# One-query attention with gradients: loads and stores described in runs of 8 KB

## The chip, the cores and the metric

The kernel runs on one core of one Trainium2 chip. The metric is the device time of one execution in microseconds. Seven executions of the kernel before took 1304.75 to 1309.08 us, median 1306.13.

The core has TensorE (matrix products, called PE in the profile; its weight loads have a row of their own, PEld), VectorE (DVE), ScalarE (ACT), GpSimd (POOL) and SyncE (SP). Sixteen transfer engines move data between the chip's large memory (DRAM) and the on-chip memory SBUF, which has 128 partitions. A transfer is started by an instruction on SyncE or GpSimd and then runs by itself; a semaphore tells when all of it has landed. The transfer engines carry it out in packets, and the profile has a record of each.

## The reference

Attention of one query per head over 8192 keys, forward and backward:

```python
B, H, Sq, Sk, D = 2, 32, 1, 8192, 128      # bfloat16
scores = einsum("bhqd,bhkd->bhqk", q, k) * D ** -0.5
p      = softmax(scores)
out    = einsum("bhqk,bhkd->bhqd", p, v)
dq, dk, dv = vjp(grad_out)                  # gradients of q, k and v
```

There are 64 heads. `k`, `v`, `dk` and `dv` each hold 134 MB, so 268 MB are read and 268 MB written. Everything else is small. With `P` the probabilities and `dS` the gradient of the scores, a row of `dv` is `P` times `grad_out`, and a row of `dk` is `dS` times `q`: both are outer products of a long vector and a vector of 128.

## The kernel before

**Tiles.** Two heads that follow one another in memory form a pair; there are 32 pairs. The 16384 rows of a pair's `k` (or `v`) are laid over the 128 partitions, 128 rows to each, so partitions 0 to 63 hold the first head and 64 to 127 the second. A row has 128 elements of 2 bytes, so a partition's share is 32 KB. It is one contiguous run in DRAM and one contiguous run in the partition, and the whole tile `kvt` is 4 MB. The view of DRAM in this form is made at line 67 (`g p n d`: pair, partition, row, element).

**Buffers.** SBUF has room for six such tiles (`NTILE`), so for three pairs. `slot_of` (line 80) gives the tile of pair i the buffer that pair i-3 used. The gradient is written over the input in the same buffer: `dv` over `v` and `dk` over `k` (`outer`, line 426). A buffer's life is therefore load, compute, overwrite, store, and then the load of a tile three pairs later.

**Transfers.** `load` (line 85) starts loads on SyncE, one transfer of 4 MB for a tile. The very first tile comes in four pieces of 1, 1, 2 and 4 chunks of 16 rows a partition (0.5, 0.5, 1 and 2 MB). `outer` starts the stores on GpSimd (line 446), one transfer of 4 MB when the last of a tile's eight chunks has been overwritten. The last pair's stores are cut finer: `dv` in two of 2 MB, `dk` in pieces of 2, 1, 0.5 and 0.5 MB (`last_v` and `last_k`, lines 453 and 454). Neither engine does much else, and each works through its transfers in program order. A load waits until the store of the tile before it in its buffer has landed.

**Work on a tile.** For a chunk of 16 rows a partition, TensorE transposes 16 blocks of 128 x 128 (line 183), ScalarE copies them out (line 185), and TensorE multiplies them with the query or with `grad_out` (line 194). That gives the scores and the products with `grad_out`. VectorE and ScalarE turn them into `P` and `dS` in steps between chunks (lines 203 to 363). TensorE then accumulates the output and `dq` over the same rows (line 376), VectorE gathers the accumulators (`pick`, line 385) and writes the outer products into the tile (line 432).

**Order.** The order of the work is written by hand. The loop at line 457 runs over chunks, 16 to a pair, and starts each stage of the earlier pairs at a fixed distance behind the transposes. Every instruction is pinned to this order on its engine (`pin`). The loads of pair i+3 are issued in the loop after the last outer product of pair i (lines 469 to 472).

Of the kernel before, what the change touches and what calls it, by code (L numbers as in the profile page):

```python
# [17 lines left out]
NG = 2  # L18
GH = 2
NTILE = 6  # L20


@with_exitstack
def kernel(
# [27 lines left out]
    load_eng = nc.sync  # L52
    store_eng = nc.gpsimd
    pin = tc.keep_in_program_order
# [25 lines left out]
    def slot_of(i, w):  # L80

        n = 2 * i + w
        return n if n < NTILE else slot_of(i - NTILE // 2, 1 - w)

    def load(i, w, pieces=(NCH,)):
        h = pairs_[i]
        t = kvp.tile([P, NT, D], BF16, tag=f"kv{slot_of(i, w)}", name="kvt")
        h.tile[w] = t
        src = (v_v if w else k_v)[i]
        c = 0  # L90
        for m in pieces:
            n0, n1 = c * CH, (c + m) * CH
            pin(load_eng.dma_start(out=t[:, n0:n1, :], in_=src[:, n0:n1, :]))  # L93
            c += m

    load(0, 0, (1, 1, 2, 4))

    qd_nat = evp.tile([P, CH, P], BF16, tag="ev", name="qd_nat")
    for w, a in enumerate((q, grad_out)):
        pin(load_eng.dma_start(out=qd_nat[:BH, w, :], in_=a.rearrange("b h s d -> (b h s) d")))  # L100

    load(0, 1)
    for j in range(1, min(NTILE // 2, NP)):
        load(j, 0)
        load(j, 1)
# [17 lines left out]
    for g in groups:  # L123
# [3 lines left out]
            out=par[g : g + CW], in_=rows.rearrange("p b h -> p h b"), axis=AX.X  # L127
# [298 lines left out]
    def outer(i, w, c, ends):  # L426

        h = pairs_[i]
        n0 = c * CH
        shape = [P, CH, D // 2, 2]  # L430
        pin(
            nc.vector.tensor_tensor(  # L432
                out=h.tile[w][:, n0 : n0 + CH, :].rearrange("p n (e t) -> p n e t", t=2),
                in0=h.qb[w][:]
                .rearrange("p (e t) -> p e t", t=2)
                .unsqueeze(1)
                .to_broadcast(shape),
                in1=h.pair[w][:, n0 : n0 + CH, :].unsqueeze(2).to_broadcast(shape),
                op=ALU.mult,
            )  # L440
        )
        if c + 1 in ends:
            at = ends.index(c + 1)
            b0, b1 = (ends[at - 1] if at else 0) * CH, (c + 1) * CH
            dst = (dv_v if w else dk_v)[i]
            pin(store_eng.dma_start(out=dst[:, b0:b1, :], in_=h.tile[w][:, b0:b1, :]))  # L446

    A1 = NCH + 4
    O1 = A1 + 1
# [7 lines left out]
    for g in range(SL * NP + O0 + NCH + 4 - SL):  # L457
# [15 lines left out]
        if x := within(O1):  # L473
            outer(x[0], 1, x[1], last_v if x[0] == NP - 1 else whole)
        if x := within(O0):
            outer(x[0], 0, x[1], last_k if x[0] == NP - 1 else whole)
# [77 lines left out]
```

## Time and profile before

| | |
|---|---|
| median of seven executions | 1306.13 us |
| lowest and highest | 1304.75 and 1309.08 us |
| the profiled execution, its time | 1309.08 us |
| the profiled execution, its span | 1307.3 us |
| read from DRAM, written to DRAM | 268.47 MB, 268.47 MB |
| store of a tile, from issue to landing (median) | 39.9 us |
| load of a tile, from issue to landing (median) | 27.8 us |
| store instruction on GpSimd, line 446 (median) | 0.53 us |
| load instruction on SyncE, line 93 (median) | 0.33 us |

The span runs from the first instruction that the profiler sees to the last; the time is what the device reports for the execution. A profile page lists the busy time of each engine, then the span in 40 slices with one digit per slice for the busy share in tenths, then the transfer queues. Queue q1 carries what SyncE starts (descriptors generated in hardware) and q0 what GpSimd starts (descriptors written by software). A queue's share is the time of its packets as a part of sixteen engines' span. Packets can overlap a little on an engine, so a share over a short stretch can exceed 1.

The compute that costs most stands in these groups; columns are line, engine, operation, tiles written and read, shapes and count, then busy time in all, mean of one, and idle time of the engine just before them with what ended it:

```profile
L185 ACT COPY ev<-tp 128x2048 bf16<-128x2048 bf16 x512 | 954.5, 1866 | 289.9 <-PE tp L183 272.1
L183 PE MATMUL tp<-ident_bf,kvt 128*128 128x128 bf16 x8192 | 584.4, 228 | 124.4 <-DMA kvt<-in_k_dram 63.1
L432 DVE TENSOR_TENSOR kvt<-qb,pair 128x2048 bf16<-128x2048 bf16 x512 | 615.4, 1219 | 50.7 <-PE acc L376 47.7
```

TensorE's transposes wait 63.1 us for loads of `k` to land, and others for loads of `v`.

### The profile page before, as it was taken

The numbers are of one execution on the slowest core, as the hardware profiler recorded it, in microseconds if no ns is written. First come the engines' busy times: TensorE is split into PE (matmuls) and PEld (weight loads), VectorE is DVE, ScalarE is ACT, GpSimd is POOL, SyncE is SP. The second block draws the span as 40 slices with busy tenths as digits, with TensorE's granted clock in tenths as the row PEclk, the third lists the DMA queues.
The fourth block names the chain that finished last, engine by engine and source line by source line (L and its number), as shares of the span: only waits on it lengthen the run. The fifth ranks groups of instructions, "written<-read, shape, count | busy, mean of one in ns | idle before, by whom it ended". The sixth has DMA issues, their size and how long they took to land.

```text
span 1307.3 us, 41375 instructions
## 1 busy us (share of the span) xinstructions
PE 1144.3 (88%) x19108; PEld 847.5 (65%) x19108; DVE 850.9 (65%) x1551; ACT 984.9 (75%) x641; POOL 37.4 (3%) x76
## 2 busy tenths in 40 slices
PE   4999998888988989889898898888888989889893
PEld 4777776666766766666666666666666667667661
DVE  0688775656756667666675675656667657577566
ACT  5899987777877868777787787777777768678770
POOL 0000000000000000000000000000000000000000
PEclk9999998989989989899898998989899889899886
DMA  9999999999999999999999999999999999999968
GB/s 400 427 366 428 429 430 430 430 430 430 427 414 426 427 422 413 410 423 419 414 405 426 412 418 415 417 413 417 421 411 418 421 420 415 423 415 417 422 268 340
DMA packets 19933, 539.58 MB, mean 413 GB/s; under 512 B 2480, under 2 KB 2480, under 8 KB 2992
## 3 DMA queue, kind: packets, MB, share of 16 engines
q1 hardware_dynamic: 9968, 268.51, 49.5%
q0 software_dynamic: 9792, 268.44, 48.3%
q8 instruction: 149, 2.44, 0.7%
q14 instruction: 24, 0.20, 0.0%
HBM read 268.47 MB, written 268.47 MB: 411 GB/s over the span
## 4 chain that ended last, share of the span: by engine, by line
issue 69%; DMA 22%; PE 5%; POOL 2%; DVE 1%; SPq 0%; ACT 0%; POOLq 0%; DVEq 0%; ACTq 0%
DMA kvt<-in_v_dram 19%; DMA out_dram<-kvt 3%; PE tp L183 2%; POOL out_dram L446 2%; PE acc L376 1%; DVE kvt L432 1%; PE dpw L194 1%; PE sw L194 0%; ACT ev L185 0%; DVE sel L399 0%; POOLq L446 0%; SPq L93 0%; SPq L100 0%; PE sw L222 0%; PE sw L211 0%
## 5 line engine op out<-in xcount | busy, mean ns | idle before, releaser
L185 ACT COPY ev<-tp 128x2048 bf16<-128x2048 bf16 x512 | 954.5, 1866 | 289.9 <-PE tp L183 272.1
L183 PE MATMUL tp<-ident_bf,kvt 128*128 128x128 bf16 x8192 | 584.4, 228 | 124.4 <-DMA kvt<-in_k_dram 63.1
L432 DVE TENSOR_TENSOR kvt<-qb,pair 128x2048 bf16<-128x2048 bf16 x512 | 615.4, 1219 | 50.7 <-PE acc L376 47.7
L183 PEld LDWEIGHTS <-kvt 128*128 128x128 bf16 x8192 | 504.2, 103 | 134.5 <-DMA kvt<-in_k_dram 65.5
L194 PEld LDWEIGHTS <-ev 128*128 128x128 bf16 x8192 | 239.9, 96 | 218.6 <-issue 135.2
L376 PE MATMUL acc<-kvt,dS_pad 128*64 128x512 bf16 x1024 | 169.6, 416 | 1.6 <-DVE dS_pad L362 1.6
L376 PE MATMUL acc<-kvt,E_pad 128*64 128x512 bf16 x1024 | 170.3, 415 | 0.0
L194 PE MATMUL sw<-qdT,ev 128*128 128x2 bf16 x4096 | 142.1, 164 | 2.6 <-ACT ev L185 2.5
L194 PE MATMUL dpw<-qdT,ev 128*128 128x2 bf16 x4096 | 142.0, 164 | 1.0 <-ACT ev L185 1.0
L270 DVE CUSTOM_DVE_ANT_0 junk<-E_f,dpw 64x128 bf16<-64x128 f32 x64 | 18.3, 285 | 125.8 <-PE dpw L194 125.4
L207 DVE TENSOR_REDUCE mp<-sw 64x1 f32<-64x128 f32 x64 | 18.5, 289 | 125.0 <-PE sw L194 124.5
L446 POOL DMA_DIRECT2D out_dram<-kvt x68 | 36.3, 534 | 1258.5 <-DVE sel L393 647.7
L399 DVE SCALAR_TENSOR_TENSOR sel<-acc,diag,sel 128x128 f32<-128x128 f32 x192 | 67.3, 351 | 6.8
L376 PEld LDWEIGHTS <-dS_pad 128*64 128x64 bf16 x1024 | 37.9, 111 | 29.5 <-issue 6.4
L376 PEld LDWEIGHTS <-E_pad 128*64 128x64 bf16 x1024 | 37.2, 111 | 26.2 <-issue 5.1
L262 DVE CAST E_pad<-E_f 64x128 bf16<-64x128 f32 x64 | 15.3, 239 | 48.5 <-ACT E_f L252 48.5
L413 PE MATMUL acc<-par,sel 128*128 128x2 f32 x128 | 21.9, 241 | 10.1 <-DVE sel L399 10.1
L413 PEld LDWEIGHTS acc<-par,sel 128*128 128x128 f32 x128 | 19.7, 195 | 10.9 <-DVE sel L399 10.9
L176 DVE CAST qb<-dpw 128x128 bf16<-128x128 f32 x64 | 18.2, 284 | 13.1 <-PE dpw L167 13.1
L252 ACT ACTIVATE E_f<-sw,negm 64x128 f32<-64x128 f32 x64 | 23.2, 362 | 1.6
L352 DVE SCALAR_TENSOR_TENSOR dSu<-dpw,negdelta,E_f 64x128 f32<-64x128 f32 x64 | 22.4, 350 | 2.2
L393 DVE TENSOR_SCALAR sel<-acc,diag 128x128 f32<-128x128 f32 x64 | 22.3, 348 | 1.0
(49 smaller groups left out, 215.1 us busy)
## 6 DMA issues: line engine op xcount, KB each, us to landing
out_dram<-kvt POOLq DMA_DIRECT2D x62, 4096.0 KB, 39.9
kvt<-in_v_dram SPq DMA_DIRECT2D x32, 4096.0 KB, 27.8
kvt<-in_k_dram SPq DMA_DIRECT2D x31, 4096.0 KB, 27.9
out_dram<-kvt POOLq DMA_DIRECT2D x3, 2048.0 KB, 8.7
kvt<-in_k_dram SPq DMA_DIRECT2D x1, 2048.0 KB, 11.5
kvt<-in_k_dram SPq DMA_DIRECT2D x2, 512.0 KB, 4.4
kvt<-in_k_dram SPq DMA_DIRECT2D x1, 1024.0 KB, 6.8
out_dram<-kvt POOLq DMA_DIRECT2D x1, 1024.0 KB, 7.6
```

Of the source, the lines that this page charges most:

```text
L183: pin(nc.tensor.transpose(tp[:, t, :], src[:, c * CH + t, :], ident_bf[:]))
L185: pin(nc.scalar.copy(out=ev[:], in_=tp[:]))
L194: nc.tensor.matmul(dst[:, c * CH + t, :], lhsT=ev[:, t, :], rhs=qdT[:, w, GH * i : GH * (i + 1)], start=True, stop=True,)
L207: pin(nc.vector.reduce_max(out=h.mp[hs], in_=h.s[hs, :, g], axis=AX.X))
L252: nc.scalar.activation(out=h.E_f[hs], in_=h.s[hs, :, g], func=ACT.Exp, bias=h.negm[hs], scale=scale, accum_out=h.ld[hs, g : g + 1],)
L352: nc.vector.scalar_tensor_tensor(out=dSu[hs], in0=h.dp[hs, :, g], scalar=negdelta[hs], in1=h.E_f[hs], op0=ALU.add, op1=ALU.mult,)
L376: nc.tensor.matmul(h.acc[w][g : g + CW, :], lhsT=wts[:, n0 * GH : n0 * GH + CW], rhs=rows[:, n0 : n0 + QT, :].rearrange("p n d -> p (n d)" ...
L393: nc.vector.tensor_scalar(out=h.sel[:], in0=block, scalar1=diag[:, 0:1], scalar2=None, op0=ALU.mult)
L399: nc.vector.scalar_tensor_tensor(out=h.sel[:], in0=block, scalar=diag[:, b : b + 1], in1=h.sel[:], op0=ALU.mult, op1=ALU.add,)
L413: nc.tensor.matmul(h.acc[w][:, 0:GH], lhsT=h.sel[:], rhs=par[:], start=True, stop=True)
L432: nc.vector.tensor_tensor(out=h.tile[w][:, n0 : n0 + CH, :].rearrange("p n (e t) -> p n e t", t=2), in0=h.qb[w][:] .rearrange("p (e t) -> ...
L446: pin(store_eng.dma_start(out=dst[:, b0:b1, :], in_=h.tile[w][:, b0:b1, :]))
```

## The change

`max_dma_last_dim` caps the last dimension of a transfer's description, in bytes; a longer run is split into several of that length. The default is 64 KB, so a partition's 32 KB were one run. The change sets 8 KB for the tiles' loads and for their stores. A 4 MB transfer is then described as 128 x 4 x 4096 elements in place of 128 x 16384, with 512 runs in place of 128; a 2 MB transfer goes from 128 runs of 16 KB to 256 of 8 KB. Transfers of 1 MB and less have runs of 8 KB or 4 KB and stay as they are. The bytes, the addresses, the number of transfers, their order and their semaphores are the same, and no other instruction differs. The loads of `q` and `grad_out` and the stores of the two small outputs keep the default.

```diff
+RUN_L = 8192
+RUN_S = 8192
...
-            pin(load_eng.dma_start(out=t[:, n0:n1, :], in_=src[:, n0:n1, :]))
+            pin(
+                load_eng.dma_start(
+                    out=t[:, n0:n1, :], in_=src[:, n0:n1, :], max_dma_last_dim=RUN_L
+                )
+            )
...
-            pin(store_eng.dma_start(out=dst[:, b0:b1, :], in_=h.tile[w][:, b0:b1, :]))
+            pin(
+                store_eng.dma_start(
+                    out=dst[:, b0:b1, :], in_=h.tile[w][:, b0:b1, :], max_dma_last_dim=RUN_S
+                )
+            )
```

## The prediction

> **What bounds the kernel now.** I read the shares of the engines first, then the transfer lines of the page, then its stages, then the waits of SyncE's queue, and at last the trace's transfer records (start, duration, size and queue of every packet).
>
> ```profile
> PE 1144.3 (88%) x19108; PEld 847.5 (65%) x19108; DVE 850.9 (65%) x1551; ACT 984.9 (75%) x641; POOL 37.4 (3%) x76
> DMA  9999999999999999999999999999999999999968
> DMA packets 19933, 539.58 MB, mean 413 GB/s; under 512 B 2480, under 2 KB 2480, under 8 KB 2992
> q1 hardware_dynamic: 9968, 268.51, 49.5%
> q0 software_dynamic: 9792, 268.44, 48.3%
> ```
>
> TensorE looks busiest by its share, but the transfer engines are busy in every slice until the last two: loads (q1) take 49.5% of sixteen engines' span and stores (q0) 48.3%. By stages:
>
> ```profile
> 20.00:56.00 36.00, 33.50 (x623) 26.95 (x621) 14.29 (x30) 33.54 (x22) 0.00 (x0) 0.95 1.00 428
> ...
> 180.00:700.00 520.00, 463.57 (x7697) 342.57 (x7696) 341.05 (x620) 396.27 (x259) 13.83 (x26) 0.92 1.00 422
> 700.00:1220.00 520.00, 455.95 (x7571) 337.17 (x7567) 336.95 (x607) 389.40 (x252) 13.29 (x25) 0.92 1.00 417
> 1220.00:1260.00 40.00, 36.21 (x617) 26.72 (x614) 26.51 (x48) 31.68 (x21) 1.06 (x2) 0.93 0.92 388
> 1260.00:1271.00 11.00, 11.00 (x177) 8.30 (x174) 7.31 (x16) 8.92 (x9) 0.10 (x1) 0.88 0.21 86
> 1271.00:1307.30 36.30, 14.83 (x169) 8.35 (x168) 24.99 (x42) 5.66 (x4) 3.62 (x7) 0.71 0.84 348
> ```
>
> The last two columns are the busy share of the transfer engines and GB/s. From 180 to 1220 us that share is 1.00 while TensorE has 56 and 64 us to spare. The transfer engines stand idle in earnest in one place, between 1260 and 1271, when the last pair is computed and there is nothing to move. The queue waits close the ring:
>
> ```profile
> SPq L93 <- DMA out_dram<-kvt: 1184.7, 58, 60.0
> ...
> POOL out_dram L446 <- DVE sel L393: 647.7, 32, 24.3
> ```
>
> A load waits for the store of the tile that it overwrites (1185 us in 58 waits), so more transfer time delays every later load. The chain of waits calls 69% of the span "issue", with no cause; I trust the transfer share instead. The kernel is bound by the time its transfer packets take.
>
> **What one packet costs.** The 4 MB transfers are 128 runs of 32 KB, and the records show one packet for a run: 8064 load and 7936 store packets of 32 KB, 1000 of them per engine. Neighbours on an engine overlap by 3 to 4 ns, so I use the median step from start to start. Other sizes stand in the same trace, because the first loads and the last stores are cut smaller:
> - loads: 32 KB 1209.5 ns, 16 KB 607, 8 KB 306 (305.7 without rounding, from a duration of 309 and the overlap), 4 KB 152.
> - stores, measured where stores alone run, mostly after the last load: 32 KB 1215 ns, 16 KB 613, 8 KB 314.5 (mean 318.3), 4 KB 160.
>
> From load packets, 32 KB in four runs costs 4 x 305.7 = 1222.8 ns against 1209.5: **13.3 ns dearer**, or 4.4 ns for each added packet. In the body, store packets behave as loads do: both have a median of 1213 ns there, a step from load to store is 1210, and one from store to load 1209, so changing direction costs at most 1 ns.
>
> The Trainium skill ("DMA: Bandwidth & Descriptors", section "Why small descriptors are slow") names about 3 cycles per packet; at the 850 MHz of that page this is an estimate of 3.5 ns, 3 x 3.5 x 1000 = 10.6 us in the sum below, where the rows make it 13.3.
>
> **Which engine paces.** Between 100 and 1220 us, 445 of 7153 store packets, one in sixteen, take 1225 to 1450 ns (mean 1304). Chained by end and start they are one engine, alternating stores near 1310 and loads near 1229: (1310 + 1229)/2 - 3.5 = 1266 ns a packet. All engines together start 6335 packets of 32 KB from 700 to 1200 us, one per engine in 500,000 x 16/6335 = 1263 ns. So the slow engine sets the pace late in the body; from 140 to 290 us, with queued work still in hand, it is 1228. The others lose the difference when they run out of loads and begin the next together: 921 load packets take over 1250 ns, and all load packets together exceed 1213 by 23.9 us per engine. What stretches the slow engine follows the instructions: store packets during which fewer than 5 instructions start are longer by 29 ns on average, those with 65 or more by 140. That goes by time and not by packet, and stays.
>
> The same skill page ("Latency and other measured facts") says that engines 7 and 15 are usually slow and guesses at the descriptor rings of software transfers. The trace agrees that one engine is slow. By that guess the stretch would grow with the descriptors, and the sum would be that of the third rival; by the count of instructions it adds nothing.
>
> **The change, part by part.**
> - Loads: 63 of 4 MB go from 128 packets to 512, one of 2 MB from 128 to 256; the 512 KB and 1 MB pieces have runs of 8 KB or less already. 504 per engine x 13.3 ns = 6.7 us.
> - Stores: 62 of 4 MB and 3 of 2 MB likewise; the last three are untouched. 496 x 13.3 = 6.6 us by the load rows; by the store-only rows 496 x (1258 - 1215 = 43) = 21.3 us, and by their mean 28.8. I take the load row: those store rows come from a stretch in which all engines store at once, while in the body the 32 KB store is at the load's 1213.
> - Cover: none, up to the last load's landing near 1256 us, as the share is 1.00 through the body; after it 199 store packets of 32 KB are left (12 per engine), so the dearer row adds there at most 12 x 43 ns = 0.5 us, and the idle 1260 to 1271 us swallows part of it.
> - Issue on GpSimd: a store instruction takes 0.53 us for 128 runs, and no row shows more runs. Bounds: 0 and three times as much again, 1.6 us. It hides: a store lands 39.9 us after issue, though 8 packets alternating with loads need 16 x 1.263 = 20.2, so it waits behind another store for some 19 us. Without that cover it is 1.6 us per store, 65 times 1.6 = 104 us at the very worst. The last, small stores keep their form.
> - Issue on SyncE: 0.33 us, bound likewise 0 to 1.0 us more per load. Loads land after 27.8 us against 20.2 of work: 7.6 us of queue hide it. SyncE has nothing else behind it but the next load, which waits for a store.
> - No semaphore, buffer, order or compute instruction changes. The landing of a transfer is still the moment when its last packet is done.
>
> Sum: 6.7 + 6.6 = 13.3 us. The profiled execution took 1309.08 us around a span of 1307.3; it becomes some 1320.6 in span and 1322.4 in time. It lies 2.95 us above the median of the seven runs, 1306.13, so I forecast 1306.1 + 13.3 = **1319.4 us**, 1.0% slower.
>
> **Rivals.**
> 1. *Shorter runs remove the load stalls (faster).* When the engines start a load together, packets take up to 2.9 us; alternating with stores every 8 KB could spread them. If all of the 23.9 us went and decided the end: 1306.1 + 13.3 - 23.9 = 1295.5 us. Against: partitions and addresses keep their order, the 4 KB loads at the start have such first packets too (801, 726, 1215 ns), and while the slow engine paces, the others' stalls cost nothing. It decides once more than 13.3 us of stall is both removed and on the path.
> 2. *Stores at the dearer row.* 6.7 + 21.3 = 28.0 us, 1334 us; by the mean row 35.5 us, 1342. For it: that is how 8 KB stores were seen.
> 3. *The slow engine's stretch goes by the packet.* Its stores run 1310 - 1213 = 97 ns over; four packets would each pay that, 3 x 97 x 496 = 144 us more: 1306 + 13 + 144 = 1463 us. Against: store packets of 16 KB and 8 KB at the end have medians of 615 and 316, 4 and 7 ns over the loads' 611 and 309, though few instructions run then.
> 4. *It does nothing*: the runs adjoin in both memories, and descriptor generation could merge them, or the packets' cost could be hidden: 1306 us. Against: the changed program's transfers carry 128x4x4096 elements where they had 128x16384, and every packet size in the trace is the last dimension of its transfer.
>
> **How the numbers follow.** Forecast (1314 to 1328) 0.58; dearer stores 0.15; per-packet stretch 0.02; nothing 0.10; stalls removed 0.15. Within 0.2% (2.6 us, about what a measurement of this kernel can tell from no change) is the fourth rival: same 0.10; faster 0.15; slower 0.75. The range, 1302 to 1337, takes in the forecast, no change, half of the second rival and the nearer third of the first, and leaves out about 2 in 10. The forecast's own range is 1314 to 1328.
>
> **What would show it.** Right: about 68,000 packets, with 34,300 on q1 and 34,000 on q0; load packets of 309 ns; the share still 1.00 from 180 to 1220 us; about 418 and 413 GB/s in the two long stages; the last load landing some 13 us later and the tail after it unchanged. Store packets near 316 instead of 309 mean the second rival; loads without packets over twice the median, and a span under 1307, the first; as many packets as before, the fourth. The prediction is wrong if GpSimd's or SyncE's instructions grow by more than their queues hide, which would show as a share below 1.00 in the body.

## The result and the profile after

The changed kernel takes 1311.03 us (median of 15 runs, 1310.1 to 1312.83) against 1307.63 us for the kernel before, run beside it (median of 35, 1304.75 to 1310.5). The ratio is 1.0027, 95% interval 1.002 to 1.0034: slower, by some 3.4 us. The forecast was 1319.4 us, slower by 13.3. The side was right and the size was not. The profiled execution took 1312.37 us around a span of 1310.6 us.

The transfer lines of the page and the same six stages as before (the last columns are PE clock, busy share of the transfer engines, GB/s):

```profile
DMA packets 68445, 539.58 MB, mean 412 GB/s; under 512 B 2480, under 2 KB 2480, under 8 KB 2992
q1 hardware_dynamic: 34288, 268.51, 49.8%
q0 software_dynamic: 33984, 268.44, 48.9%
```

```profile
20.00:56.00 36.00, 33.08 (x646) 26.59 (x643) 15.18 (x32) 34.73 (x23) 0.25 (x1) 1.00 1.01 417
180.00:700.00 520.00, 460.70 (x7591) 340.56 (x7593) 335.63 (x609) 390.32 (x254) 18.61 (x25) 0.92 1.01 421
700.00:1220.00 520.00, 460.61 (x7634) 340.01 (x7632) 341.30 (x617) 393.98 (x257) 19.34 (x26) 0.92 1.01 413
1220.00:1260.00 40.00, 36.38 (x597) 26.88 (x597) 26.30 (x48) 30.41 (x20) 1.49 (x2) 0.91 1.01 417
1260.00:1271.00 11.00, 9.34 (x137) 6.76 (x138) 3.99 (x9) 6.84 (x8) 0.00 (x0) 0.84 0.61 258
1271.00:1310.60 39.60, 21.38 (x242) 12.10 (x239) 28.53 (x49) 9.36 (x6) 4.51 (x7) 0.69 0.79 324
```

The packets became what they were meant to be: 34,288 and 33,984 in place of 9968 and 9792. The loss shows where only loads run (417 GB/s against 428) and late in the body (413 against 417). From 180 to 700 us it is barely there (421 against 422). At the end the picture turns round. Between 1220 and 1271 us the transfer engines had room before (0.92 and 0.21 busy) and are busier now (1.01 and 0.61). Work that came late fell into time that had been idle.

The trace's transfer records tell how much. Tiles of 4 MB that the engines had moved, loads and stores together (a packet under way counts by the part of its time that has passed):

```
time in the span, us     before     after    behind
 600                      59.74     59.42     0.32
 900                      89.32     88.93     0.39
1140                     113.13    112.54     0.59
1230                     122.03    121.33     0.70
1260                     124.76    124.27     0.49
1270                     125.00    124.95     0.05
```

Late in the body a 4 MB tile takes 10.1 us (8 packets per engine at 1263 ns), so 0.70 tiles are 7.1 us. By 1230 us the forecast's price came to 13.0 us (122 tiles x 8 packets per engine x 13.3 ns), so little more than half of it shows. By 1270 us nearly all of the lag is caught up, because the old kernel's transfers had run dry. Of the delay 3.3 us of span is left, carried by the compute after the last load. The chain of waits names that load in both kernels (start, duration):

```profile
1223.08 33.63 DMA kvt<-in_v_dram
```

```profile
1233.71 27.90 DMA kvt<-in_v_dram
```

The first line is the kernel before, the second the changed one. The load starts 10.6 us later, but takes 5.7 us less, and lands at 1261.6 instead of 1256.7 us: 4.9 us later, where the prediction had some 13. From the end of the last load packet to the end of the span it was 52.1 us and is now 49.8; the prediction had that tail unchanged.

GpSimd's store instructions did grow. The line's view (minimum, median and maximum in ns) now reads 743 ns for 512 runs; with 128 runs it was 531. Before and after:

```profile
L446 POOL DMA_DIRECT2D out_dram<-kvt x68: 531/531/673, 56.7 to 1295.9; - x68
```

```profile
L453 POOL DMA_DIRECT2D out_dram<-kvt x68: 532/743/885, 55.7 to 1299.7; - x68
```

### The profile page after: what moved, and what is told of

It reads as the page before. It is cut to its first block, busy times and chain, and to the rows that moved or that the text cites. A ratio compares the mean times of both kernels' runs of the same rounds, so it can differ in the third digit from the quotient of the medians.

```text
span 1310.6 us, 41375 instructions
## 1 busy us (share of the span) xinstructions
PE 1151.0 (88%) x19108; PEld 851.0 (65%) x19108; DVE 850.7 (65%) x1551; ACT 984.8 (75%) x641; POOL 51.1 (4%) x76
## 3 DMA queue, kind: packets, MB, share of 16 engines
q1 hardware_dynamic: 34288, 268.51, 49.8%
q0 software_dynamic: 33984, 268.44, 48.9%
## 4 chain that ended last, share of the span: by engine, by line
issue 86%; DMA 7%; POOL 3%; DVE 1%; PE 1%; SPq 0%; POOLq 0%; ACT 0%; DVEq 0%; ACTq 0%
DMA kvt<-in_v_dram 4%; DMA out_dram<-kvt 3%; POOL out_dram L453 3%; DVE kvt L438 1%; PE tp L189 1%; PE acc L382 0%; PE dpw L200 0%; POOLq L453 0%; ACT ev L191 0%; DVE sel L405 0%; SPq L96 0%; SPq L106 0%; PE acc L419 0%; DVE dSu L358 0%; DVE sel L399 0%
## 5 line engine op out<-in xcount | busy, mean ns | idle before, releaser
L382 PE MATMUL acc<-kvt,E_pad 128*64 128x512 bf16 x1024 | 173.8, 423 | 0.0
L453 POOL DMA_DIRECT2D out_dram<-kvt x68 | 50.1, 736 | 1248.5 <-DVE kvt L438 620.7
L182 DVE CAST qb<-dpw 128x128 bf16<-128x128 f32 x64 | 18.2, 284 | 13.6 <-PE dpw L173 13.6
L346 DVE TENSOR_SCALAR negdelta<-dpw,rl 128x1 f32<-128x1 f32 x32 | 7.0, 218 | 27.2 <-PE dpw L306 27.1
## 6 DMA issues: line engine op xcount, KB each, us to landing
kvt<-in_v_dram SPq DMA_DIRECT2D x32, 4096.0 KB, 27.8
kvt<-in_k_dram SPq DMA_DIRECT2D x31, 4096.0 KB, 27.9
kvt<-in_k_dram SPq DMA_DIRECT2D x1, 2048.0 KB, 11.4
```

What stands on the lines that cost most here:

```text
L382: nc.tensor.matmul(h.acc[w][g : g + CW, :], lhsT=wts[:, n0 * GH : n0 * GH + CW], rhs=rows[:, n0 : n0 + QT, :].rearrange("p n d -> p (n d)" ...
```

## The experiments

Each run was timed against the kernel before on the same chip; ratios compare these. Between chips the kernel before itself differs, with medians from 1306.81 to 1309.88 us, so a difference of 2 or 3 us between runs on two chips is read by ratios or left undecided. Where the text says "late", it means a packet's duration over the undisturbed one of its size (159, 309, 611 and 1213 ns for 4, 8, 16 and 32 KB), from the transfer records.

**One side alone.** Two kernels set one constant of the change and leave the other at 32 KB.

```diff
-RUN_S = 8192
+RUN_S = 32768
```

> Loads in 8 KB runs, stores in 32 KB runs. Theory A (the added packets cost 4.4 ns each on the path, 13.3 us for both sides; fewer load stalls give about 6 us of it back, and idle transfer time at the end hides about 3): half of the packets, 6.7 us, is added. And the engines alternate queues packet by packet, so stores take four times the bytes of loads while both wait; the last load lands later against the stores, and the idle time at the end grows: 1310 to 1322 us. Theory B (the packets' cost lies beside slack of the engines and only the issue of stores on GpSimd, 0.53 to 0.74 us, is on the path): stores keep their form, so 1306 to 1308 us.

```diff
-RUN_L = 8192
+RUN_L = 32768
```

> Stores in 8 KB runs, loads in 32 KB runs. Theory A: 6.7 us more for the packets, but loads now take four times the bytes of stores while both wait, so the last load lands earlier and more of the stores fall into the idle time at the end (about 11 us): 1298 to 1309 us, and a larger store backlog when the last load lands than the 3.3 tiles of before. Theory B (only the issue of stores on GpSimd is on the path): the whole difference of the change, 1310 to 1312 us.

Short loads alone took 1324.36 us, ratio 1.0122 (1.0097 to 1.0147), a little above theory A's range. Short stores alone took 1308.80 us, 0.9995 (0.9982 to 1.0008), just inside theory A's. Theory B falls on both: the store instructions were 533 ns in the slow one and 743 ns in the one that costs nothing. The lists of transfers show the other half, the sharing between queues (last column: us from issue to landing). Short loads first, then short stores:

```profile
out_dram<-kvt POOLq DMA_DIRECT2D x62, 4096.0 KB, 18.0
kvt<-in_v_dram SPq DMA_DIRECT2D x32, 4096.0 KB, 46.2
```

```profile
out_dram<-kvt POOLq DMA_DIRECT2D x62, 4096.0 KB, 49.9
kvt<-in_v_dram SPq DMA_DIRECT2D x32, 4096.0 KB, 18.8
```

Before, they were 39.9 and 27.8. An engine takes a packet from each queue in turn, whatever its size, so the side with longer runs gets its bytes through first. The records show it between 150 and 300 us, wherever an engine's packets can be followed by their ends and starts: with short loads exactly one load of 8 KB stands between two stores of 32 KB (662 times of 662, where sharing by bytes would put four), and with short stores exactly one store between two loads (596 of 597). With short loads the tiles arrive late, TensorE loses 8 us between 60 and 180 us (111.99 us busy against 119.92), and the last load lands at 1266 us. The stretch from 60 to 180 us, in the kernel before and with short loads:

```profile
60.00:180.00 120.00, 119.92 (x2137) 89.57 (x2136) 94.55 (x171) 110.53 (x75) 3.72 (x7) 1.00 0.98 413
```

```profile
60.00:180.00 120.00, 111.99 (x1962) 83.75 (x1960) 85.52 (x155) 101.22 (x68) 3.19 (x6) 0.96 0.99 411
```

With short stores the last load lands at 1253 us and 4.2 tiles are left to store in place of 3.7. They use the idle time at the end (share 0.67 from 1260 to 1271 us, where it was 0.21), and that can pay for the added packets; no run separates it.

**Other lengths on both sides.**

```diff
-RUN_L = 8192
-RUN_S = 8192
+RUN_L = 4096
+RUN_S = 4096
```

> Loads and stores in 4 KB runs, seven added packets for each 32 KB in place of three. Theory A: 4.4 ns x 7000 = 31 us more work per engine, less 6 to 10 us of stalls and 3 us of cover at the end: 1323 to 1330 us. Theory B (packets hidden, issue on GpSimd on the path): the store instruction grows again by some 0.3 us, so 1312 to 1316 us.

```diff
-RUN_L = 8192
-RUN_S = 8192
+RUN_L = 16384
+RUN_S = 16384
```

> Loads and stores in 16 KB runs, one added packet for each 32 KB. Theory A: 4.4 us more work per engine; if the relief of the stalls goes with the length of the runs it may give 2 to 5 back: 1304 to 1310 us. Theory B: 1307 to 1309 us, with store instructions of 0.6 us.

4 KB: 1322.37 us, 1.0099 (1.0081 to 1.0116), 0.6 us below theory A's range and well above B's. 16 KB: 1304.89 us, 0.9966 (0.9951 to 0.998), *faster* than before and inside theory A's range alone. Run again on another occasion:

> The whole kernel with loads and stores in runs of 16 KB once more, on another chip perhaps. Theory C: below the kernel before by 2 to 6 us, a ratio of 0.995 to 0.999, as the slow engine's pace says (5.5 us). Rival: the gain seen once was the chip's or the runs' spread: a ratio of 1.000 to 1.004, as the price of the packets alone would give (5.6 us).

1304.13 us, 0.9962 (0.9946 to 0.9977): inside theory C's range, though the pace that was its reason does not hold up (below). The gain of 0.3 to 0.4% is there on both chips. The records show what shorter runs give back. Loads over 250 ns late, and what they add per engine:

```
runs              such loads    us per engine    all lateness, loads + stores, us per engine
32 KB                575            20.9              24.6 + 9.0
16 KB                505            16.7              22.1 + 6.4
16 KB, again         500            17.1              22.4 + 6.1
 8 KB                391            12.8              19.3 + 7.8
 4 KB                 32             0.8               5.2 + 16.1
 8 KB, loads only    376             9.4              19.8 + 12.8
 8 KB, stores only   355            11.3              15.8 + 15.4
```

The two runs with 16 KB agree to 0.1 us in all lateness. With one side short the sum hardly falls (33.6 to 32.6 and 31.2): the loads are less late and the stores later.

If the stalls are on the path, the transfers should lag by the added price less the lateness that went. The price here uses the undisturbed steps of these traces: 1209.4, 607.1, 305.9 and 155.3 ns for 32, 16, 8 and 4 KB, so 32 KB cost 4.7, 14.1 and 33.0 ns more in the three shorter lengths. All in us per engine, up to 1230 us of the span, against the kernel before:

```
runs      price    lateness that went    price less that    lag measured
16 KB       4.6           5.0                -0.4            -1.1 (both runs)
 8 KB      13.8           7.0                 6.8             7.1
 4 KB      32.2          13.2                19.0            15.9
```

For 16 and 8 KB the last two columns agree within a microsecond, for 4 KB within some 3.

**The price of a packet by itself.** All computation is left out; every tile is loaded and stored again.

```diff
-    load(0, 0, (1, 1, 2, 4))
...
+    for j in range(min(NTILE // 2, NP)):
+        load(j, 0)
+        load(j, 1)
+    for i in range(NP):
+        for w in (1, 0):
+            store(i, w)
+            if i + 3 < NP:
+                load(i + 3, 1 - w)
```

> All computation left out: each tile is loaded and stored again unchanged, with the same six buffers and queues, in runs of 32 KB. Theory A: 1000 packets of 32 KB per engine at a step of 1209.5 ns, and some 10 to 35 us around them and in load stalls: 1220 to 1245 us. If the slow engine of the kernel before is slow because instructions run, no engine is slow here; if it is slow by its stores alone, the pace stays near 1263 ns a packet and the time near 1275 us.

> The same copy without computation, in runs of 8 KB. Theory A: 13.3 us over the copy in runs of 32 KB, less what the stalls give back, so 6 to 14 us over it. Theory B (the cost of packets is hidden): within 3 us of it.

32 KB took 1250.11 us, somewhat over the range: a copy has 1024 large packets per engine, not 1000. 8 KB took 1261.26 us, 11.2 us more, inside theory A's range. The windows of the two copies, 32 KB first (GpSimd's busy time, PE clock, share, GB/s):

```profile
180.00:700.00 520.00, 13.69 (x26) 1.00 1.00 434
```

```profile
180.00:700.00 520.00, 19.23 (x26) 1.00 1.01 428
```

By the records a step of 32 KB takes 1209.4 ns in the first and 1223.5 ns in the second, so the 13.3 ns of the forecast are right to a nanosecond; 1024 times 13.3 are 13.6 us, and the last store packet ends 13.7 us later (1258.0 us against 1244.3). There is no slow engine and hardly a late packet here: 1.7 us per engine in all, against 33.6 in the kernel before.

**What makes one engine slow.** Beside the copy, TensorE multiplies constant tiles that no one needs; otherwise nothing is computed.

```diff
+    for j in range(19000):
+        pin(nc.tensor.matmul(pst[:], lhsT=wt[:], rhs=mv[:], start=True, stop=True))
```

> The copy in runs of 32 KB without the kernel's computation, with 19,000 independent small products (128 x 128 on constant tiles, as many as the kernel has matrix products) on TensorE beside it. Theory C (one engine is slowed while many instructions run, and paces): one engine's packets again run at some 1263 ns in place of 1210, and the time rises from 1250 us by 25 to 45 us, as long as TensorE keeps issuing. Theory D (the slow engine comes from the stores beside VectorE's and ScalarE's work on the tiles, or from waits of the kernel): no slow engine, 1249 to 1253 us.

> The same with runs of 8 KB. Theory C, with the stretch of the slow engine smaller for short packets (54 ns per 32 KB fell to 47 between the two kernels, against 13.3 ns for the packets): 3 to 10 us over the copy with TensorE in runs of 32 KB, less than the 11.2 us between the copies without it. If the stretch went by time alone: 11 to 14 us over it. Theory D: 11 us over it, and no slow engine.

> The copy in runs of 32 KB beside 5,000 products of 128 x 512 on TensorE, about as long in busy time as the 19,000 small ones, with a quarter of the instructions. If the number of instructions slows the engine: a quarter of the stretch, some 1255 to 1262 us. If TensorE's work itself does: as with the small products, 1275 to 1295 us.

> The copy in runs of 16 KB with 19,000 small products on TensorE beside it, without the kernel's computation. Theory C with a stretch that shrinks for shorter packets: the slow engine's pace in the whole kernel was 1263.5 ns per 32 KB in runs of 32 KB, 1258 in runs of 16 KB and 1270 in runs of 8 KB, so this copy lies 2 to 6 us below the one in runs of 32 KB (1295.4): 1289 to 1294 us. If the stretch goes by time alone: 5.6 us above it, near 1301 us.

Medians: 1295.43 us (32 KB), 1301.88 (8 KB), 1262.50 (32 KB with 5,000 large products), 1296.91 (16 KB). The first lies 0.3 us above what theory C allowed, the third 0.5 us above its range. TensorE's instructions add 45.3 us to a copy that has nothing to do with them (on another chip, where the kernel before took 1306.81 us against 1308.0). With about a quarter of the instructions and as much busy time it is 12.4 us. First the 19,000 small products, then the 5,000 large ones:

```profile
PE 1068.8 (83%) x19000; PEld 1064.7 (82%) x19000; DVE 0.5 (0%) x3; POOL 34.2 (3%) x68
```

```profile
PE 1081.9 (86%) x5000; PEld 489.8 (39%) x5000; DVE 1.1 (0%) x3; POOL 34.2 (3%) x68
```

So theory C holds and D falls: one engine's packets are stretched along with the number of instructions that run, not with TensorE's busy time and not with the stores alone.

What comes with the number of instructions is their own transport too. Queue q8 carries instructions, in packets of 16 KB (packets, MB, share of sixteen engines), with 19,000 products and with 5,000:

```profile
q8 instruction: 148, 2.42, 0.7%
```

```profile
q8 instruction: 39, 0.64, 0.2%
```

These packets do not make the engine slow by taking turns on it. With 19,000 products its sequence of some 158 packets between 100 and 300 us can be followed in the same way: 140 of them are stretched, and none of the 28 instruction packets of that time stands among them.

The slight lateness between 100 and 300 us, put on one engine, in ns for each 32 KB that it moves:

```
                     32 KB    16 KB    8 KB
the kernel            54.0     54.5    54.0
copy with 19,000      53.2     53.8    51.3
copy with 5,000       14.5
copy alone             0.4              0.0
```

Here my reason in the expectation of the 8 KB copy fell, though its number came true. I had read a shrinking stretch (54 to 47) from the medians of the chained engine. Taken over all packets of a stretch in which hardly a load stalls, it does not shrink: 54 ns in the kernel for all three run lengths, 51 to 54 in the copy.

The slow engine's own work can now be added up for the copies. TensorE runs until 1084 us of the span with long runs and until 1064 with the two shorter ones. In that time 32 KB take 1209.4 + 53.2 = 1262.6 ns in long runs, 1214.1 + 53.8 in runs of 16 KB, and 1223.5 + 51.3 in runs of 8 KB, and afterwards the plain step. With 1024 packets of 32 KB from 1.8 us on, the last store should end at 1286, 1291 and 1297 us. The records have 1290.5, 1292.8 and 1298.3: some 4, 2 and 1 us on top. The late loads stand in the same order, with 13.4, 10.2 and 7.3 us of lateness per engine. That narrows the 11.2 us between the plain copies to 6.5 here.

The 16 KB copy took 1.5 us more than the 32 KB copy where I had expected 2 to 6 less, or 5.6 more: both ranges missed. The two were on different chips; against the kernel before on its own chip the ratios are 0.9907 (0.989 to 0.9924) and 0.9917 (0.9901 to 0.9932), so no difference between them is shown.

**Holding stores back at the end.** Runs of 16 KB, and 4 KB for the stores of the pairs before the last.

```diff
-max_dma_last_dim=RUN_S
+max_dma_last_dim=RUN_T if NP - 3 <= i < NP - 1 else RUN_S
```

> The whole kernel with loads and stores in runs of 16 KB, but the stores of pairs 29 and 30 (from 0) in runs of 4 KB, so that the last two loads take four times the bytes of these stores. Theory A: the last load lands 4 to 10 us earlier than with 16 KB alone (1254 us of the span), the idle time of the transfer engines near 1260 us shrinks, and the time is 2 to 6 us below it: 1299 to 1303 us against 1304.9. Rival: the work on TensorE and VectorE after the last load already sets the end, and the deferred stores pile up behind it: 1305 to 1310 us.

The last load landed at 1244.4 us, 9.8 us earlier than in the first run with 16 KB, as wanted. The time did not gain: 1304.57 us, ratio 0.9987 (0.9978 to 0.9996). In microseconds that equals the runs with 16 KB alone, but on this chip the kernel before was faster too (1306.81 us), and by the ratios it is some 0.2% worse than they are (0.9966 and 0.9962). At that landing 4.75 tiles were left to store in place of 3.5. The last outer products ended some 6 us earlier, but the last store landed at 1302.6 us against 1301.9. Theory A is wrong, and the rival is nearer, though the time lies 0.4 us below its range and only its second half fits: compute ended earlier, and the deferred stores ended last.

## Why the prediction was right or wrong

- *The bound.* Right. The transfers' packets bound the kernel, and a copy without any computation takes 1250 us of the 1306.
- *The price of the packets*, 13.3 ns for 32 KB. Right: 14.1 ns between the copies, 11.2 us in their times.
- *Stores by the load row*, not by the dearer one of the end. Right: 8 KB store packets have a median of 309 ns in the body. Rival 2 falls.
- *One engine paces late in the body, and its stretch goes by time.* Right for the two kernels compared: 54 ns for each 32 KB in all three lengths between 100 and 300 us. From 700 to 1200 us the mean step went from 1262.8 to 1277.1 ns, 14.3 more, and both values are the slow engine's own (1209.4 + 54.0 and 1223.5 + 54.0) to a nanosecond. Runs of 16 KB do not fit: 1263.6 and 1262.7 ns there against 1214.1 + 54.5 = 1268.6. Rival 3 falls, and with it the guess of the Trainium skill ("DMA: Bandwidth & Descriptors", "Latency and other measured facts") that the descriptor rings do it. Four times the descriptors left the stretch at 54 ns, and the copy with the same rings and no instructions has none.
- *"While the slow engine paces, the others' stalls cost nothing."* **This step was wrong** for the kernel as a whole. It set rival 1 aside and put the stalls at nothing for all of the time up to the last load, though the prediction itself had the slow engine pace only late in the body. Up to 1230 us the packets' price was 13.8 us by the measured steps, lateness fell by 7.0 us per engine (from 32.3 to 25.3), and the transfers fell behind by 7.1 us: the stalls that went were on the path to about their mean. It happened early. From 180 to 700 us the mean step was 1249.8 ns, below the slow engine's 1263, so that engine did not yet pace; there the step rose by 1.5 ns only, while lateness fell from 11.4 to 6.9 us. From 700 to 1200 us the step rose by the whole price, as the sentence would have it, though lateness fell by 2.3 us there too. Rival 1 was right in kind, in a quarter of its size: the loads' lateness fell by 5.3 us of 24.6, all lateness by 6.5 of 33.6.
- *Cover: none up to the last landing, at most 0.5 us after it.* **Too strict.** I looked only at what the tail adds, and not at what its idle time could take from the body's delay. The lag of 7.1 us at 1230 us was 3.3 us at the end. The last load's 33.6 us became 27.9, and the transfer engines had been idle for 8.7 of the 11 us before 1271.
- *Issue on GpSimd and SyncE hidden.* Right: 0.53 to 0.74 us for a store, and the kernel with short stores alone, whose stores take as long to issue, is not slower.

Together: of a price of 13.8 us some 6.7 came back before 1230 us, by fewer late packets, and 3.8 after it, in the time that had been idle. That leaves 3.3 us of span, and 3.4 in the medians. The two returns are read from the records; no run takes one away and leaves the other.

What stays open. The gain with 16 KB has two parts: its transfers are 1.1 us ahead at 1230 us, as price and lateness nearly cancel (4.6 against 5.0), and the other 2.4 and 3.7 us of its spans come after that. From the last load packet to the end it takes 49.5 us in both runs; with 8 and 4 KB it is 49.8 and 50.3, and before it was 52.1. So this shorter end goes with all three lengths, and why is not shown; the one profile of the kernel before is also 1.5 us above the median of its 35 runs. Why short runs make loads stall less was not tried by itself either.

## What to carry to other kernels

Price a change of packet length per packet, from sizes that stand in the same trace, and then ask what the lateness of the old packets was worth: it does not stay constant, and it can return half of the price. Look also at where transfers run dry near the end, because that time absorbs delay from the stage before it. The two queues share an engine packet by packet, so unequal run lengths are a priority between loads and stores; equal runs of 16 KB were best here, 0.3 to 0.4% below 32 KB, and 8 KB loads against 32 KB stores the slowest, 1.2% above.

## What was not expected of the hardware

- Instructions slow one transfer engine: 38,000 of TensorE's small instructions beside an independent copy cost 45.3 us of 1250, and 10,000 cost 12.4. What it is about an instruction that slows the engine is not shown. All traces here carry the profiler's records of these instructions, so it stays open whether it is so without them.
- An engine alternates between the queues by packets and not by bytes: with 8 KB loads against 32 KB stores, a store lands after 18.0 us and a load after 46.2; with lengths exchanged it is 49.9 and 18.8.
- A store instruction on GpSimd takes 0.53, 0.72, 0.74 and 0.88 us for 128, 256, 512 and 1024 runs: the first doubling costs most, and 0.74 us was not on the path.
